# Loading the gate weights by partitions instead of by halves of their rows

## The chip, the core and the metric

The kernel runs on one core of one Trainium2 chip. The metric is the device time of one execution in microseconds (us). A core has five engines with instruction queues of their own: TensorE (PE: matmuls, and PEld: its weight loads), VectorE (DVE), ScalarE (ACT), GpSimd (POOL) and SyncE (SP). Sixteen DMA engines beside them move data between HBM and the on-chip memory SBUF, whose 128 partitions are the first axis of every tile. In this kernel DMAs are issued by SP and ACT; each of the two has a queue of its own, which the profile calls q1 (SP) and q10 (ACT).

## The reference

One decoding step of eight sequences. x is normalised; an attention over the last 2048 cached keys and values (32 query heads on 8 cached heads) gives s; a gated unit on the same normalised x gives g; the output is x + s * g. Everything stored is bfloat16.

```python
xn = _layernorm(x)                                   # 8 x 512
q = xn @ wq                                          # 32 heads of 128
scores = einsum("bhqd,bhkd->bhqk", q, k) * Dh ** -0.5    # k, v: last 2048 rows
o = einsum("bhqk,bhkd->bhqd", softmax(scores), v)
s = o.reshape(B, Sq, Hq * Dh) @ wo
h = sigmoid(xn @ w_gate) * (xn @ w_up)               # 512 x 1792 each
g = silu(h @ w_down)
return x + s * g
```

## The kernel before, in words

All that is read is some 81 MB: the weights, and for each of 8 sequences two loads of keys and two of values, 2048 KB each. Every large load fills all 128 partitions with one contiguous run per partition, which the DMA trace shows as one packet: 14336 bytes for the weights w_gate and w_up (four rows of 1792 numbers), 16384 bytes for keys and values. A DMA over 128 partitions is spread over all 16 DMA engines, eight packets on each, and each engine closes its part with a 4-byte completion write. The landing that a reader of the tile waits for is the sixteenth of these.

The order of the work is written out by hand. A list `todo` holds the loads in the order in which they are to be issued; `pump()` issues from its head as long as the pool that the load goes to has room (5 buffers for keys, 4 for values; the weights borrow these buffers), and `free()` gives a buffer back after its last reader. Nearly all loads are issued by SP (`q0`), in this order: x (L149), half of w_gate (L151), w_up, w_down and wq in two parts (L99, `load_rows`), a remainder of w_down called wd_part in three small pieces (L187), then keys and values (L89, `load_cache`), and last wo in four parts (L99). ACT (`q1`) issues two only: the other half of w_gate (L151) and a second copy of x, x4_sb (L157; the profile leaves digits out and calls it x_sb), which is needed only at the very end (L750).

What is computed from them, in order: normalisation of x (L216 to L254), the gate's 16 matmuls (L295, `hidden("wg_sb")`), its sigmoid on ACT (L308), the same 16 matmuls with w_up (L295), their product (L312), the down projection (L348; its last three matmuls need wd_part), silu (L371, L375), the queries (L385), then for each sequence the transposes of the keys (L481), scores (L500), softmax (L515 to L548) and values (L597), and at the end the output projection (L719, L733), the sum with x (L748, L750) and the store (L751).

`hidden` goes through the four rows `kt` of each partition, so that its first eight matmuls read rows 0 and 1 and its last eight rows 2 and 3. A further wait matters below: eight completion semaphores serve all DMAs in turn, so the ninth and later DMAs of SP's queue each wait until the DMA eight places before them has landed. The three wd_part pieces (L187) wait for ACT's part of w_gate, for x and for SP's part of w_gate, and the first load of keys (L89) for x4_sb, the next two for w_up and w_down.

The function that is changed, with what calls it:

Of the kernel before, what the change touches and what calls it, by code (L numbers as in the profile page):

```python
# [10 lines left out]
def kernel(  # L11
# [14 lines left out]
    P = 128  # L26
# [6 lines left out]
    KT = D // P  # L33
# [47 lines left out]
    q0, q1 = nc.sync, nc.scalar  # L81
# [65 lines left out]
    def want_first():  # L147
        t = vpool.tile([P, KT, F], bf16, name="wg_sb", tag="v")
        q0.dma_start(out=x_bf[:], in_=A_x.flatten_outer_dims())  # L149
        for q, r0 in ((q1, 0), (q0, KT // 2)):  # L150
            q.dma_start(  # L151
                out=t[:, r0 : r0 + KT // 2, :],
                in_=B_w_gate.rearrange("(p r) n -> p r n", r=KT)[
                    :, r0 : r0 + KT // 2, :
                ],
            )
        q1.dma_start(  # L157
            out=x4_sb[::S, :],
            in_=A_x.flatten_outer_dims().rearrange("b (j c) -> j b c", c=P),
        )  # L160
        for r in range(KT):
            weights[("wg_sb", r)] = t[:, r, :]

    later("v", want_first)
    want_rows("wu_sb", B_w_up, "v", KT, 0, KT)

# [38 lines left out]
    for t0, t1 in ((0, KS), (KS, 26), (26, 30), (30, RT)):  # L205
# [11 lines left out]
        out=perm[:].rearrange("k (l p) -> k l p", l=G),  # L217
        in_=ident[:].rearrange("k (p l) -> k l p", l=G),
# [13 lines left out]
        out=rstd[:], in_=mv[:, 1:2], func=AF.Sqrt, bias=eps_t[:], scale=1.0  # L232
# [4 lines left out]
        out=xn_bf[:],  # L237
# [8 lines left out]
    for kt in range(KT):  # L246
        nc.tensor.transpose(  # L247
            out=xnT_ps[:, kt, :],
            in_=xn_bf[:].rearrange("b (p kt) -> b kt p", kt=KT)[:, kt, :],
# [11 lines left out]
    for t in p_buf:  # L261
# [7 lines left out]
        out=own_q[:], in_=ident_f[:].rearrange("k (h q) -> k q h", q=NDQ), axis=AX.X  # L269
# [3 lines left out]
        out=sel_z[:], in_=ident_f[:].rearrange("k (j z) -> k z j", z=Z), axis=AX.X  # L273
# [4 lines left out]
    for p0, n, x0, x1, s0, a in PARTS:  # L278
        for x in range(x0, x1):
            nc.vector.tensor_copy(  # L280
                out=sel_part[:, x, p0 : p0 + n].rearrange("k (a e) -> k a e", a=a),
                in_=ident[:, s0 : s0 + n * (x1 - x0)].rearrange(
                    "k (e x a) -> k x a e", x=x1 - x0, a=a
                )[:, x - x0],
# [6 lines left out]
    def hidden(name):  # L291
# [21 lines left out]
        out=h_sb[:].rearrange("k t p -> k p t"),  # L313
# [7 lines left out]
        out=hT_sb[:].rearrange("k t z -> k (t z)"),  # L321
        in_=h_sb[:].rearrange("k t p -> k (t p)"),
# [79 lines left out]
    for x in range(Hkv // JQ):  # L402
        for r in range(rep):
            nc.tensor.transpose(  # L404
                out=qT_ps[:, x, r, :], in_=q_bf[:, x, r, :], identity=ident[:]
            )
        nc.vector.tensor_copy(
            out=qm_sb[:, :, x * JQ : (x + 1) * JQ, M0 : M0 + rep],
            in_=qT_ps[:, x].rearrange("d r (j z) -> d z j r", z=Z)[:, ::S],
# [11 lines left out]
    for i in range(NQ):  # L421
        nc.vector.tensor_copy(
            out=turn_rows[:].rearrange("k (i j l r) -> k i j l r", i=NQ, j=NJ, l=G)[
                :, i
            ],
            in_=ident[:].rearrange("k (l j i r) -> k i j l r", i=NQ, j=NJ, l=G)[:, i],
        )
        nc.vector.reduce_sum(
            out=sel_den[:, i * Hh : (i + 1) * Hh].rearrange("k (l r) -> k l r", l=G),
            in_=ident_f[:].rearrange("k (l j i r) -> k i l r j", l=G, j=NJ, i=NQ)[:, i],  # L430
            axis=AX.X,
        )
    for e in range(2):
        nc.vector.reduce_sum(
            out=sel_out[:, e, :].rearrange("k (i h) -> k i h", i=NQ),
            in_=ident_f[:].rearrange(
                "k (i m e h) -> k e i h m", i=NQ, m=NJ // 2, e=2
            )[:, e],
# [9 lines left out]
        out=sel_res[:],  # L448
# [6 lines left out]
        out=sel_sum[:], in_=sel_den[:].unsqueeze(2).to_broadcast([P, Hq, NDQ])  # L455
# [287 lines left out]
    for t in range(KS, RT):  # L743
# [8 lines left out]
        out=out.flatten_outer_dims().rearrange("b (j c) -> j b c", c=P),  # L752
        in_=y_bf[::S, :],
# [31 lines left out]
```

## Time and profile before

| | |
|---|---|
| Time, median of 3 runs | 199.54 us (199.35 to 199.58) |
| The profiled execution, its own time | 199.71 us |
| Its span, first to last instruction | 197.9 us |
| Busy in the span: PE, DVE, ACT, POOL | 154.0, 122.5, 37.6, 3.0 us |
| DMA: bytes, mean rate over the span | 81.32 MB, 411 GB/s |
| DMA packets; on SP's queue q1, on ACT's q10 | 6295; 6096 and 180 |
| Packet time as a share of 16 engines' span, q1 and q10 | 95.0% and 1.4% |
| Mean granted TensorE clock | 0.963 |

The profile gives the span; the 1.8 us between it and the execution's own time lie outside. A DMA issue in the timeline is the time the issuing engine spends on it, not the transfer; transfers are seen in the DMA rates, in the packets of the trace, and as releasers of those who wait. In the lines of the chain of waits the first number is the start, the second how long that piece of the chain took.

### The profile page before, as it was taken

What the parts mean: (1) busy time and instruction counts of PE and PEld (TensorE: products, weight loads), DVE (VectorE), ACT (ScalarE), POOL (GpSimd) and SP (SyncE); (2) the same over time, 40 slices, a digit from 0 to 9 for tenths busy, and PEclk for the clock granted to TensorE, in tenths of its full rate; (3) what the DMA queues carried; (4) which work ended last, traced back from release to release, by engine and by line L of the source; (5) the groups of instructions that cost most, each with busy time, mean ns of one, the idle gap of its engine ahead of it and who ended that gap; (6) DMA issues with size and microseconds to landing.
All of it is one profiled execution on the core that took longest, in us unless ns stands there. A gap on an engine that the chain in (4) does not pass through costs nothing.

```text
span 197.9 us, 4794 instructions
## 1 busy us (share of the span) xinstructions
PE 154.0 (78%) x2145; PEld 104.6 (53%) x2145; DVE 122.5 (62%) x234; ACT 37.6 (19%) x91; POOL 3.0 (2%) x11
## 2 busy tenths in 40 slices
PE   0434038799989999979798969996999897888652
PEld 0111014677676677647565646674667564566531
DVE  3754002999978678748675937685867774762301
ACT  3300011000710600240024000600060024082010
POOL 6000000000000000000000000000000000000000
PEclk9999999999999999999999969996999999999975
DMA  6999999999999999999999999999999999999980
GB/s 212 441 429 432 428 430 434 430 434 422 427 430 424 430 430 437 424 427 427 427 430 426 437 430 427 426 427 430 427 430 427 427 437 424 434 424 430 419 334 10
DMA packets 6295, 81.32 MB, mean 411 GB/s; under 512 B 764, under 2 KB 900, under 8 KB 1412
## 3 DMA queue, kind: packets, MB, share of 16 engines
q1 hardware_dynamic: 6096, 80.10, 95.0%
q10 hardware_dynamic: 180, 0.93, 1.4%
q8 instruction: 16, 0.26, 0.5%
q14 instruction: 3, 0.02, 0.0%
HBM read 81.02 MB, written 0.01 MB: 409 GB/s over the span
## 4 chain that ended last, share of the span: by engine, by line
DMA 72%; PE 22%; DVE 2%; ACT 1%; issue 1%; SPq 1%
DMA k_sb<-in_A_k_cache_dram 49%; DMA wo_sb<-in_A_wo_dram 11%; PE kT_ps L481 11%; DMA wd_part<-in_B_w_down_dram 9%; PE o_ps L597 4%; DMA wg_sb<-in_B_w_gate_dram 3%; PE s_ps L500 3%; PE q_ps L385 1%; PE fin_ps L733 1%; DVE kT_sb L486 1%; PE qT_ps L404 0%; PE b_ps L361 0%; PE pT_ps L571 0%; PE w_ps L348 0%; ACT q_bf L399 0%
## 5 line engine op out<-in xcount | busy, mean ns | idle before, releaser
L486 DVE COPY kT_sb<-kT_ps 128x1024 bf16<-128x1024 bf16 x128 | 85.2, 686 | 31.0 <-PE kT_ps L481 30.3
L481 PE MATMUL kT_ps<-perm,k_sb 128*128 128x128 bf16 x1024 | 76.5, 223 | 9.4 <-DMA k_sb<-in_A_k_cache_dram 9.3
L481 PEld LDWEIGHTS <-k_sb 128*128 128x128 bf16 x1024 | 59.7, 99 | 29.3 <-issue 16.5
L597 PE MATMUL o_ps<-v_sb,pT_sb 128*32 128x256 bf16 x512 | 39.8, 277 | 1.1 <-DVE o_sb L618 0.9
L500 PE MATMUL s_ps<-kT_sb,qm_sb 128*32 128x512 bf16 x256 | 26.0, 396 | 1.9 <-DVE kT_sb L486 1.9
L597 PEld LDWEIGHTS <-pT_sb 128*32 128x32 bf16 x512 | 22.0, 97 | 9.9 <-issue 3.3
L548 ACT ACTIVATE p_buf<-s_ps,nb 32x512 bf16<-32x512 f32 x32 | 21.7, 678 | 0.5
L541 ACT COPY nb<-m_ps 128x1 f32<-128x1 f32 x8 | 1.3, 159 | 88.3 <-PE m_ps L535 88.3
L571 PE MATMUL pT_ps<-turn_rows,p_buf 128*128 128x128 bf16 x128 | 10.9, 230 | 1.5 <-ACT p_buf L548 1.5
L564 DVE COPY pT_sb<-pT_ps 128x1024 bf16<-128x1024 bf16 x14 | 9.6, 687 | 3.9 <-PE pT_ps L571 3.9
L500 PEld LDWEIGHTS <-qm_sb 128*32 128x32 bf16 x256 | 6.7, 93 | 8.9 <-issue 2.5
L571 PEld LDWEIGHTS <-p_buf 128*128 128x128 bf16 x128 | 9.3, 150 | 3.4 <-ACT p_buf L548 2.1
L613 ACT ACTIVATE o_odd<-o_ps,own_col 128x128 f32<-128x128 f32 x8 | 2.9, 367 | 27.4 <-PE o_ps L597 27.4
L375 DVE TENSOR_TENSOR gg_sb<-sigb,b_ps 128x128 f32<-128x128 f32 x1 | 0.3, 286 | 11.7 <-ACT sigb L371 11.7
L348 PE MATMUL w_ps<-wd_part,hP_sb 52*32 52x512 bf16 (+1 forms) x3 | 0.6, 597 | 7.9 <-DMA wd_part<-in_B_w_down_dram 7.9
L548 ACT ACTIVATION_READ_ACCUMULATOR p_buf<-s_ps,nb 32x1 f32 x32 | 5.9, 184 | 0.0
L515 DVE TENSOR_REDUCE st<-s_ps 128x1 f32<-128x512 f32 x8 | 5.5, 682 | 0.5 <-PE s_ps L500 0.5
L640 DVE SCALAR_TENSOR_TENSOR own<-m_ps,inv,own_q 128x128 f32<-128x128 f32 x8 | 2.8, 346 | 3.3 <-PE m_ps L631 3.3
L348 PEld LDWEIGHTS <-hP_sb 52*32 52x32 bf16 (+1 forms) x3 | 0.1, 97 | 8.8 <-issue 8.8
L618 DVE SCALAR_TENSOR_TENSOR o_sb<-o_ps,own_col,o_odd 128x128 f32<-128x128 f32 x8 | 2.7, 339 | 3.0 <-ACT o_odd L613 3.0
L247 PE MATMUL xnT_ps<-ident,xn_bf 8*128 8x8 bf16 x4 | 0.3, 176 | 5.4 <-DVE xn_bf L236 5.4
L295 PEld LDWEIGHTS <-xnT_sb 128*32 128x32 bf16 x32 | 1.1, 119 | 6.3 <-issue 5.8
(80 smaller groups left out, 68.7 us busy)
## 6 DMA issues: line engine op xcount, KB each, us to landing
k_sb<-in_A_k_cache_dram SPq DMA_DIRECT2D x16, 2048.0 KB, 30.8
v_sb<-in_A_v_cache_dram SPq DMA_DIRECT2D x16, 2048.0 KB, 29.8
wq_sb<-in_A_wq_dram SPq DMA_DIRECT2D x2, 2048.0 KB, 18.1
wo_sb<-in_A_wo_dram SPq DMA_DIRECT2D x1, 2048.0 KB
wu_sb<-in_B_w_up_dram SPq DMA_DIRECT2D x1, 1792.0 KB, 10.5
wd_sb<-in_B_w_down_dram SPq DMA_DIRECT2D x1, 1664.0 KB, 14.0
wo_sb<-in_A_wo_dram SPq DMA_DIRECT2D x1, 1280.0 KB, 21.7
wg_sb<-in_B_w_gate_dram ACTq DMA_DIRECT2D x1, 896.0 KB
```

The lines of the kernel that those rows point to most:

```text
L385: nc.tensor.matmul(q_ps[x][Z * j : Z * (j + 1), :], lhsT=xnT_sb[:, kt, :], rhs=weights[("wq_sb", kt)][:, g * rep * Dh : (g + 1) * rep * Dh ...
L481: nc.tensor.transpose(out=kT_ps[:, c, :], in_=k_sb[:, j * CU + h * CH + c, :], identity=perm[:],)
L486: nc.vector.tensor_copy(out=kT[(b, u)][:, h * CH : (h + 1) * CH, :], in_=kT_ps[:])
L500: nc.tensor.matmul(s_ps[b][NR * l : NR * (l + 1), :], lhsT=qm_sb[:, b, i * G + l, o : o + Z], rhs=t[:, :, PG * l : PG * (l + 1)], start=(u ...
L515: nc.vector.reduce_max(out=st[b][:], in_=s_ps[b][:], axis=AX.X)
L548: nc.scalar.activation(out=p_buf[b % 2][rows, :, l, :], in_=s[rows, :].rearrange("k (c p) -> k p c", p=PG), func=AF.Exp, bias=nb[rows, :], ...
L564: copy(out=pT[b][:, h * CH : (h + 1) * CH, :], in_=pT_ps.pop(h)[:])
L571: nc.tensor.transpose(out=pT_ps[h][:, c, :], in_=p_buf[b % 2][:, :, :, h * CH + c].rearrange("k p l -> k (p l)"), identity=turn_rows[:],)
L597: nc.tensor.matmul(o_ps[rows, b % 2, :].rearrange("k (e d) -> k e d", e=2), lhsT=pT[b][:, c, rows], rhs=v[:, m, c], start=(c == 0), stop=( ...
L613: nc.scalar.mul(out=o_odd[:], in_=o_ps[:, b % 2, Dh:], mul=own_col[:, 1:2])
L618: nc.vector.scalar_tensor_tensor(out=o_of[b // 2][:, b % 2, :], in0=o_ps[:, b % 2, :Dh], scalar=own_col[:, 0:1], in1=o_odd[:], op0=ALU.mul ...
L640: nc.vector.scalar_tensor_tensor(out=own[:], in0=m_ps[:, b % 2, P : 2 * P].rearrange("p (q t) -> p q t", q=NDQ), scalar=inv[y][:, b % 2 : ...
```

## The change

Both DMAs of w_gate change their shape, and nothing else does. Before, ACT's queue carried rows 0 and 1 of all 128 partitions and SP's queue rows 2 and 3: 128 packets of 7168 bytes each. Now ACT's queue carries all four rows of partitions 0 to 111, 112 packets of 14336 bytes, and SP's queue all four rows of partitions 112 to 127, 16 packets of 14336 bytes. All other instructions keep their order on each engine. Since every row now lies in both parts, the first weight load of the gate's matmuls waits for SP's part and the first matmul for ACT's; before, the first eight matmuls waited for ACT's half alone.

```diff
-        for q, r0 in ((q1, 0), (q0, KT // 2)):
+        for q, p0, p1 in ((q1, 0, P - 16), (q0, P - 16, P)):
             q.dma_start(
-                out=t[:, r0 : r0 + KT // 2, :],
-                in_=B_w_gate.rearrange("(p r) n -> p r n", r=KT)[
-                    :, r0 : r0 + KT // 2, :
-                ],
+                out=t[p0:p1],
+                in_=B_w_gate.rearrange("(p r) n -> p r n", r=KT)[p0:p1],
             )
```

## Prediction

> **What bounds the kernel now.** I read the page's slices and chain first, then the stretches, the end of the chain, the start of the timeline, and last SP's own waits. From the page, 40 slices of 4.95 us each:
>
> ```profile
> DMA  6999999999999999999999999999999999999980
> GB/s 212 441 429 432 428 430 434 430 434 422 427 430 424 430 430 437 424 427 427 427 430 426 437 430 427 426 427 430 427 430 427 427 437 424 434 424 430 419 334 10
> ...
> DMA 72%; PE 22%; DVE 2%; ACT 1%; issue 1%; SPq 1%
> ```
>
> The reader sees transfers at 90% or more in every slice but the first and the last two, at some 428 GB/s throughout. The busy times by stretch say the same (the last two columns are DMA share and GB/s):
>
> ```profile
> 1.60:7.60 6.00, 1.23 (x12) 0.50 (x13) 3.56 (x9) 2.86 (x3) 1.90 (x6) 1.00 0.99 375
> 7.60:30.00 22.40, 7.03 (x63) 2.50 (x66) 7.27 (x18) 1.41 (x3) 0.00 (x0) 1.00 1.01 430
> 30.00:190.00 160.00, 142.63 (x2005) 99.64 (x1994) 111.05 (x206) 32.77 (x84) 0.00 (x0) 0.98 1.01 428
> ```
>
> So from 1.7 us to 190 us the DMA engines never pause; only the first 6 us run below the rate (375 GB/s). The chain of waits, from 185 us on, shows who ends last:
>
> ```profile
> 170.37 21.74 DMA wo_sb<-in_A_wo_dram
> 192.11 0.04 issue
> 192.15 1.86 PE fin_ps L733 x56
> 194.01 0.02 issue
> 194.04 0.43 PE fin_ps L733 x7
> ```
>
> The last matmuls wait for the last part of wo. Its 16 completion writes land between 190.37 and 193.99 us, and the matmuls start at 194.04. Each DMA engine has its own share of every load and none takes another's, so **the kernel ends 4 us after the slowest of the 16 engines**, and time that this engine loses anywhere, also in the first 6 us, is not made up. That makes the start of the queue the only place where this change can act. SP's waits show that the queue is fed far ahead: SP waits 124.5 us in all for buffers that the transposes free (L481), while a load of keys lands 30.8 us (median) after its issue and takes about 4.9 us of the queue (2.1 MB at 428 GB/s).
>
> **The change part by part.**
>
> *Bytes and packets.* The bytes are the same. A packet of 7168 bytes starts 0.268 us after the one before it on its engine, one of 14336 bytes 0.532 us (w_up's packets). Each engine had sixteen of the first kind and gets eight of the second: 8 x (2 x 0.268 - 0.532) = **-0.03 us**. Each engine's share is the same if 112 partitions are spread over 16 engines, seven each, as 128 are (eight each, 16 completions). The trace shows 16 engines for 128 partitions, 8 for the 8 rows of x, 5 and 4 where the outer count is 5 and 4; none for 112. If it were 14 engines with eight, those would carry nine packets with SP's one, +0.53 us. [...]
>
> *Where SP's sixteen packets go.* This is the term that decides. Every large load of before writes all 128 partitions at once. SP's new DMA writes 16 neighbouring partitions, one packet per engine, from 16 engines at once: 229,376 bytes. At the rate of all other loads it would take each engine one packet, 0.53 us. No row shows such a load, so its cost has bounds. Below: nothing more; a lead of one engine over another might even hide it. Above: if eight neighbouring partitions take no more than the one engine's rate at which they are fed in full-width loads, 16 packets go two at a time, 8 x 0.532 = 4.26 us, +3.7 us. The nearest row is the load of x (L149), the only one with many engines on few partitions: eight packets of 1024 bytes into partitions 0 to 7, from 1.687 to 1.805 us in the packet records, 8192 bytes in 0.118 us, 69 GB/s for eight partitions. Its packets took 44 ns, no more than the 46 ns of wd_part's of the same size, but its completions landed 0.36 to 0.41 us after their writes were started, against 0.33 to 0.36 us for those of ACT's half of w_gate: a first sign of queueing at 69 GB/s. I take this as the rate: 16 partitions get 139 GB/s, 229,376 bytes take 1.65 us, which is **+1.12 us** over the 0.53 us of a full-width load. Sixteen engines share the delay, and the next loads (w_up, w_down) wait behind it on each engine, since the queue is served in order.
>
> *ACT's 112 partitions.* With seven per engine, an engine's seven no longer are one group of eight; neighbours meet for one packet at each side. Below, nothing; above, two packets at half speed, +1.06 us. By the x row eight partitions take 69 GB/s, more than the 54 GB/s of two engines, so I take nothing.
>
> *When the gate weights land, and who waits.* Costed at nothing. The start of the timeline:
>
> ```profile
> 0.74 0.39 ACTq L151 DMA_DIRECT2D wg_sb<-in_B_w_gate_dram  x1
> 1.18 0.37 SPq L151 DMA_DIRECT2D wg_sb<-in_B_w_gate_dram  x1
> ...
> 7.88 0.94 PE L295 MATMUL h_ps<-wg_sb,xnT_sb 128*32 128x448 bf16 x8 [0.85 <-DMA wg_sb<-in_B_w_gate_dram]
> ...
> 8.86 0.54 ACT L308 ACTIVATE sig<-h_ps 128x448 f32<-128x448 f32 x1 [2.97 <-PE h_ps L295]
> ...
> 12.12 1.69 PE L295 MATMUL h_ps<-wu_sb,xnT_sb 128*32 128x448 bf16 x16 [3.30 <-DMA wu_sb<-in_B_w_up_dram]
> ...
> 26.75 0.61 PE L348 MATMUL w_ps<-wd_part,hP_sb 60*32 60x512 bf16 x3 [7.90 <-DMA wd_part<-in_B_w_down_dram]
> ```
>
> Now all 16 gate matmuls (2 x 0.94 = 1.88 us) wait for both parts. ACT's packets came first in before (x aside, q1's first packet on any engine starts at 4.514 us, when that engine is through with q10's); seven packets more, 3.7 us from 1.8 us with some 0.7 us lost to slow first packets, and then SP's, land at about 7.1 to 8.2 us. The gate is through by 10.1 us instead of 8.82, the sigmoid by 10.6; w_up's matmuls wait for w_up until 12.12 anyway, later if the queue is later. If SP's queue were served in turn with ACT's, ACT's part would land at about 10.3 us (1.8 + 0.7 + 14 x 0.532 + 0.35) and the gate end at 12.2; the down projection would still be done by about 20, and its last three matmuls wait for wd_part until 26.75: that is the cover, some 8 us. Without it the price would be 1.3 to 3.4 us.
>
> *The queue behind.* On SP, three pieces of wd_part wait for the two parts of w_gate and x, and behind them the first keys wait for x4_sb. x4_sb follows ACT's part in its queue and comes in eight turns with SP's packets on each of four engines, so it lands at 6.2 + 8 x 0.55 = 10.6 us or so, not 8.8. SP's first keys are then issued about 2 us later, at 11. The engines have w_up, w_down and wq before them until 25.8 us (wq's last completion), so nothing runs dry. ACT issues two DMAs as before; POOL and DVE get nothing new.
>
> **Sum.** 199.71 (this execution) + 1.12 - 0.03 = 200.8 us; the execution lies 0.17 us above the median, so the forecast is **200.6 us**.
>
> **The rivals.** About 0.2% (0.4 us) is what a measurement of this kernel can tell from no change.
>
> 1. *The sixteen packets share nothing* (27%). [...] Then only -0.03 us is left: 199.5 us. [...]
>
> 2. *Faster: the slowest engine loses its early lag* (10%). In before, ACT's first packets take 272 to 939 ns instead of 272, until about 3.6 us. The completions of ACT's half land at 4.87 to 5.32 us for fourteen engines and at 5.57 and 5.69 for the last two; for w_up it is 11.29 to 11.70, then 11.95 and 12.07. One such engine could be the one that ends last: 193.99 us, 0.35 us behind the next (193.64). If the loss is per packet, half as many packets halve it, and the two fall in with the rest: 199.54 - 0.35 - 0.03 = 199.2 us. It decides only if the sixteen packets cost less than that 0.35 us. That slow packets stop by time, not by count, on all engines, speaks against it.
>
> 3. *Harder sharing* (26%). If the engines' packets meet four to a path instead of at the x row's rate, four take 4 x 0.532 = 2.13 us, +1.6 us, and 201.1 us; with ACT's neighbours meeting too, up to +1.06 more, 202.2. For it: at 428 GB/s over 16 engines each engine always fills its own partitions at 26.8 GB/s, and nothing shows that eight partitions can take more for long. Against it: x's 69 GB/s. [...]
>
> The forecast (x's rate; 199.95 to 201.1 us) has 37%. Slower is then 37 + 26 = 63%, same 27%, faster 10%. The range leaves out the lower half of the faster case and the hardest sharing (beyond 202.2, up to the bound of +3.7 us, some 8%): 199.2 to 202.2 us.
>
> **What would show each step right or wrong.** Right: SP's sixteen 14336-byte packets, or those around them on the same engines, take clearly longer than 535 ns; the completions of w_up spread and land some 1 us after 12.07; the slice of the first 6 us falls below 375 GB/s; the last part of wo lands about 1 us after 193.99 and the chain's last matmuls start as much later, with the stretch from 30 to 190 us still at 428 GB/s. Wrong, rival 1: all those packets take 535 ns and w_up lands at 12.0. Rival 2: the same, and the last two completions of w_up close up to the rest. Rival 3: w_up lands 1.6 us late or more. The cover would be wrong if L348's last matmuls no longer waited for wd_part, and the queue if a slice after the first fell below 9 tenths. The whole reading would be wrong if w_up landed late and the last wo didn't.

## The result, and the profile after

The changed kernel takes **203.09 us** (median; 202.91 to 203.76) against 199.45 us for the kernel before measured beside it: 1.0179 times as long, 95% interval 1.0163 to 1.0195. It is slower, as forecast, but by 3.6 us instead of 1.1, and outside the range. The profiled execution took 202.91 us with a span of 200.6 us, 2.7 us more than the span of before's profiled execution, 197.9 us. That one was long: the 71 executions of before that were recorded beside the experiments have spans of 197.2 to 197.8 us, median 197.5. The changed kernel's four have 200.5 to 201.2, median 200.6. So the span grew by 3.1 us. The time outside the span differs from one execution to the next (1.7 to 3.2 us in before's, 1.8 to 3.3 in the changed kernel's).

The page's slices and chain of the changed kernel (40 slices of 5.0 us):

```profile
DMA  6999999999999999999999999999999999999980
GB/s 185 226 410 428 441 428 428 425 435 425 430 428 431 428 431 421 435 428 431 425 431 426 431 425 435 426 431 418 438 428 435 418 435 428 438 415 438 422 351 29
...
DMA 57%; PE 34%; ACT 3%; DVE 3%; SPq 1%; issue 1%
```

The reader should compare the two upper lines. The engines are as busy as before in every slice, but in the second they move 226 GB/s where before they moved 441, and in the third 410 instead of 429. From the fourth slice on both run at some 428 GB/s. Busy is the time that packets took; the packets took longer: ACT's 112 packets took 922 ns on average and 99 of them over 560, where packets of the same size (w_up's) took 535 in before. (In the last line the chain of waits now runs less over DMAs and more over PE, but the two lines above it show that the DMA engines still don't pause.) By stretches (DMA share and GB/s are the last two columns), first the changed kernel, then the kernel before for the one stretch not shown yet:

```profile
1.60:7.60 6.00, 0.29 (x4) 0.20 (x4) 3.56 (x9) 2.86 (x3) 1.90 (x6) 1.00 1.09 257
7.60:13.60 6.00, 1.69 (x16) 0.76 (x17) 4.00 (x14) 0.51 (x1) 0.00 (x0) 1.00 0.89 323
13.60:33.00 19.40, 5.93 (x55) 2.09 (x58) 3.26 (x4) 0.90 (x3) 0.00 (x0) 1.00 1.01 431
33.00:190.00 157.00, 140.02 (x1989) 98.15 (x1982) 110.05 (x204) 32.79 (x84) 0.00 (x0) 0.99 1.01 429
```

```profile
7.60:13.60 6.00, 2.42 (x24) 0.78 (x23) 4.01 (x14) 0.54 (x1) 0.00 (x0) 1.00 0.98 419
```

257 GB/s instead of 375 for 6 us are 0.71 MB too few, 323 instead of 419 another 0.58 MB: 1.28 MB in all, which at 428 GB/s are 3.0 us. That is the whole loss of the span, and it arises before 13.6 us. The start of the changed kernel's timeline:

```profile
0.74 0.40 ACTq L151 DMA_DIRECT2D wg_sb<-in_B_w_gate_dram  x1
...
1.20 0.33 SPq L151 DMA_DIRECT2D wg_sb<-in_B_w_gate_dram  x1
...
11.36 1.69 PE L293 MATMUL h_ps<-wg_sb,xnT_sb 128*32 128x448 bf16 x16 [5.66 <-DMA wg_sb<-in_B_w_gate_dram]
...
15.10 1.69 PE L293 MATMUL h_ps<-wu_sb,xnT_sb 128*32 128x448 bf16 x16 [2.06 <-DMA wu_sb<-in_B_w_up_dram]
...
29.90 0.61 PE L346 MATMUL w_ps<-wd_part,hP_sb 60*32 60x512 bf16 x3 [8.07 <-DMA wd_part<-in_B_w_down_dram]
```

w_up's matmuls start 2.98 us later than before, the matmuls that wait for wd_part 3.15 us later, and they still wait 8.07 us: nothing but the transfers has become late. In the packet records w_up's sixteenth completion lands at 15.06 instead of 12.07 us, w_down's at 18.98 instead of 16.08, wq's second at 28.64 instead of 25.78. The end of the chain:

```profile
173.08 21.88 DMA wo_sb<-in_A_wo_dram
194.96 0.04 issue
195.00 1.84 PE fin_ps L731 x56
196.84 0.00 issue
196.84 0.43 PE fin_ps L731 x8
```

The last completions of wo lie between 193.57 and 196.80 us, the last 2.81 us later than before. What the engines lost in the first 13 us they lost for good.

### The profile page after: what moved, and what is told of

Its sections match the earlier page's. It is cut to its first block, busy times and chain, and to the rows that moved or that the text cites. A ratio compares the mean times of both kernels' runs of the same rounds, so it can differ in the third digit from the quotient of the medians.

```text
span 200.6 us, 4795 instructions
## 1 busy us (share of the span) xinstructions
PE 152.2 (76%) x2145; PEld 103.8 (52%) x2145; DVE 122.2 (61%) x234; ACT 37.6 (19%) x91; POOL 3.0 (1%) x11
## 4 chain that ended last, share of the span: by engine, by line
DMA 57%; PE 34%; ACT 3%; DVE 3%; SPq 1%; issue 1%
DMA k_sb<-in_A_k_cache_dram 32%; PE kT_ps L479 17%; DMA wo_sb<-in_A_wo_dram 11%; DMA wd_part<-in_B_w_down_dram 8%; PE o_ps L595 6%; DMA wg_sb<-in_B_w_gate_dram 5%; PE s_ps L498 5%; ACT p_buf L546 2%; PE pT_ps L569 2%; PE q_ps L383 1%; PE fin_ps L731 1%; SPq L185 1%; DVE kT_sb L484 1%; ACT L546 1%; PE qT_ps L402 0%
## 5 line engine op out<-in xcount | busy, mean ns | idle before, releaser
L479 PE MATMUL kT_ps<-perm,k_sb 128*128 128x128 bf16 x1024 | 75.7, 221 | 10.5 <-DMA k_sb<-in_A_k_cache_dram 10.5
L479 PEld LDWEIGHTS <-k_sb 128*128 128x128 bf16 x1024 | 59.0, 99 | 30.1 <-issue 15.9
L293 PE MATMUL h_ps<-wg_sb,xnT_sb 128*32 128x448 bf16 x16 | 1.7, 573 | 5.7 <-DMA wg_sb<-in_B_w_gate_dram 5.7
L310 DVE TENSOR_TENSOR h_sb<-sig,h_ps 128x448 bf16<-128x448 f32 x1 | 2.1, 2077 | 4.9 <-PE h_ps L293 4.9
```

What stands on the lines that cost most here:

```text
L293: nc.tensor.matmul(ps[Z * j : Z * (j + 1), :], lhsT=xnT_sb[:, kt, :], rhs=weights[(name, kt)][:, j * FC : (j + 1) * FC], start=(kt == 0), ...
L310: nc.vector.tensor_tensor(out=h_sb[:].rearrange("k t p -> k p t"), in0=sig[:, :FC].rearrange("k (p t) -> k p t", t=FT), in1=u_ps[:].rearra ...
L479: nc.tensor.transpose(out=kT_ps[:, c, :], in_=k_sb[:, j * CU + h * CH + c, :], identity=perm[:],)
```

## The experiments

The most telling number of each run is when w_up's last completion lands, since all of the gate's load is ahead of it: 12.07 us in before. It is read from one execution, the traced one. Spans of one kernel mostly differ by 0.2 to 0.7 us, and before's traced one was 0.4 us longer than its median, so small differences between landings don't count by themselves; the median span of all executions is given where it matters. Times are medians; each ratio is against the kernel before on the same chip.

| run | gate's load | w_up landed, us | time, us | ratio, 95% interval |
|---|---|---|---|---|
| before | two halves of the rows | 12.07 | 199.45 | |
| changed | 112 and 16 partitions, two queues | 15.06 | 203.09 | 1.0163 to 1.0195 |
| e1 | 128 partitions, one load on ACT | 12.44 | 199.97 | 1.0020 to 1.0048 |
| e2 | 112 and 16, both on SP | 15.41 | 203.01 | 1.0156 to 1.0195 |
| e3 | 64 and 64, two queues | 15.81 | 203.22 | 1.0150 to 1.0289 |
| e4 | 112 alone | 13.80 | 200.99 | 1.0056 to 1.0098 |
| e12 | e4's bytes over 128 partitions | 11.57 | 199.24 | 0.9960 to 1.0001 |
| e5 | before, and 16 neighbours | 13.70 | 201.23 | 1.0062 to 1.0119 |
| e6 | before, and 16, eight apart | 12.69 | 200.22 | 1.0014 to 1.0051 |
| e7 | before, and 16, seven apart | 12.69 | 199.96 | 1.0012 to 1.0040 |
| e8 | before, and the same bytes over 128 | 12.51 | 199.82 | 1.0013 to 1.0038 |
| e9 | 112 as seven loads of 16 | (see there) | 210.68 | 1.0537 to 1.0588 |
| e10 | 128 partitions, one load on SP | 12.70 | 200.42 | 1.0041 to 1.0074 |
| e11 | one load for each row | 12.07 | 199.77 | 1.0006 to 1.0034 |

**e1, one full-width load** in place of the loop over two.

```diff
+        q1.dma_start(out=t[:], in_=B_w_gate.rearrange("(p r) n -> p r n", r=KT))
```

> All of w_gate in one load of 128 partitions with packets of 14336 bytes on ACT's queue; SP's queue starts with w_up. Theory A (engines that write few neighbouring partitions at once share a path into SBUF): no load is narrow any more, so the time is that of before, 199.4 us within 0.4, w_up lands at about 12.0 us, and the packets from 4 us on take 535 ns. Theory B (two queues served in turn cost time): w_up's packets now take turns with ACT's, so it is slow, 201 us or more. Theory C (large packets at the cold start cost time): slow too, above 201 us.

Theory B falls, and C as the whole cause: two queues in turn with large packets lose 0.37 us at w_up, not 3. But 199.97 us is more than A's 199.4 within 0.4, and the median span is 198.0 us against 197.5: a small part of the loss, 0.37 of 2.99 us at w_up, 0.5 of 3.1 us in the span, comes with this one large load. All but two of w_up's 128 packets took 535 ns or 2 ns less.

**e2, both loads on one queue.** Only `q1` becomes `q0`, so that SP issues both.

> The changed kernel's two loads (112 and 16 partitions), both on SP's queue, one behind the other. Theory A: still slow, 201.0 to 202.5 us, w_up lands 1.5 to 2.5 us after 12.07; a little less than with two queues since the narrow load no longer mixes with the rest. Theory B: back to 199.4 us. Theory C: as slow as the changed kernel, 203 us.

203.01 us and w_up at 15.41: as slow as the changed kernel. With e1, the split by partitions is the cause, not the second queue. The loss is larger than A's expected 1.5 to 2.5 us.

**e3, halves of the partitions.**

```diff
+        for q, p0, p1 in ((q1, 0, P // 2), (q0, P // 2, P)):
```

> Partitions 0 to 63 on ACT's queue, 64 to 127 on SP's, packets of 14336 bytes, four of each per engine. Theory A: sixteen engines write only half of the partitions, two engines to each path; served one after the other each packet takes twice as long, 8.5 us instead of 4.3, so 203 to 204 us; less (down to 201.5) where the two queues are served in turn. If only the sixteen-partition load is a burden: 199.4 us. Theories B and C: 203 us, as the changed kernel.

203.22 us, +3.74 us at w_up: within A's 203 to 204. (One of the four executions took 206.16 us, so the interval is wide.) ACT's 64 packets took 990 ns on average in place of 535, and none took less than 560; SP's 64 behind them took 1070 on average, which is twice 535, as theory A had it. A load need not be as narrow as 16 partitions to be slow.

**e4, the 112 partitions alone.** SP's load is left out; the gate's matmuls read 112 partitions.

> ACT's 112 partitions alone; the load of partitions 112 to 127 and their share of the gate's sum (64 of 512 rows) are left out, so 0.53 us less per engine is to be moved than in before. If the sixteen partitions alone cause the loss, as the prediction took it: 198.9 us, w_up at 11.5 us. Theory A with neighbours meeting (two packets per engine at half speed): 199.5 to 200.2 us, w_up at 12.3 to 12.9 us. If most of the loss is in the 112: 201 us or more.

200.99 us, w_up at 13.80: later than theory A's 12.3 to 12.9. Most of the loss is here, where the prediction had put nothing. The median span, 199.1 us, says the same.

**e12, the control for e4**, run last, with the same bytes over the full width.

```diff
+        part = 7 * F // 2
+        q1.dma_start(
+            out=t[:].rearrange("p r n -> p (r n)")[:, :part],
+            in_=B_w_gate.rearrange("(p r) n -> p (r n)", r=KT)[:, :part],
+        )
```

> The control for e4: the same 1.6 MB of w_gate in one load on ACT's queue, but full width: the first 12544 bytes (three and a half rows) of all 128 partitions, eight packets per engine instead of seven of 14336. Left out are the last half row and its two matmuls (two of sixteen). If the loss of e4 comes from 112 partitions not being dealt out as 128 are (theory A): no loss but that of the cold start, w_up at 11.8 to 12.0 us (e1's 12.44 less 0.53), 199.3 to 199.6 us. If it comes from the bytes, the queue or the packet size: w_up at 13.8 and 201.0 us as in e4.

w_up at 11.57 us against 13.80, and 199.24 against 200.99 us: the same number of bytes on the same queue is 2.23 us later at w_up, and 1.75 us longer in time and in the median span (199.1 against 197.35), when it goes to 112 partitions and not to 128. The packets of e12 are smaller (12544 bytes), but e1's had e4's 14336 bytes, and it lost 0.37 us. The stretches show it, e4 first, then e12:

```profile
1.60:7.60 6.00, 0.29 (x4) 0.30 (x5) 3.56 (x9) 2.86 (x3) 1.90 (x6) 1.00 1.00 274
7.60:13.60 6.00, 1.68 (x16) 0.64 (x16) 4.01 (x14) 0.54 (x1) 0.00 (x0) 1.00 0.99 351
```

```profile
1.60:7.60 6.00, 0.29 (x4) 0.31 (x5) 3.27 (x9) 2.86 (x3) 1.67 (x6) 1.00 0.96 360
7.60:13.60 6.00, 3.36 (x30) 1.27 (x30) 4.58 (x15) 0.54 (x1) 0.00 (x0) 1.00 1.01 429
```

Both have a DMA share of about 1; e4 moves 274 and 351 GB/s with it, e12 360 and 429. In e4, 107 of ACT's 112 packets took over 560 ns, the 112 took 839 on average, and 92 of w_up's 128 behind and between them took over 560 ns too.

**e5 to e8, what partitions a load of 16 goes to.** Each adds to the kernel before one load behind SP's half of w_gate, 131,072 bytes into a tile `extra` that nothing reads; e5, e6 and e7 read the same rows of HBM.

```diff
+        q0.dma_start(out=extra[P - 16 : P], in_=G[P - 16 : P, :4096])      # e5
+        q0.dma_start(out=extra[0:121:8], in_=G[P - 16 : P, :4096])         # e6
+        q0.dma_start(out=extra[0:106:7], in_=G[P - 16 : P, :4096])         # e7
+        q0.dma_start(out=extra[:, :512], in_=G[:, :512])                   # e8
```

(G is w_gate as partitions by 7168 numbers.)

> The kernel before with one more load behind SP's half of w_gate, into a tile that nothing reads: 8192 bytes to each of the 16 partitions 112 to 127, one packet per engine (0.31 us of each engine at the usual rate). Theory A1 (eight neighbours share a path): eight packets to a path, 2.4 us, w_up lands at 14.2 us instead of 12.07, 201.5 us. [...] Theory D (the sixteen packets are slow because they read neighbouring rows of HBM): slow as well, and by the same amount in the two runs that read the same rows into other partitions. No sharing: 12.4 and 199.7 us.

> As e5, the same rows of HBM, but into partitions 0, 8, 16 to 120. Theory A1: every packet has a path of its own: 12.4 us for w_up's landing, 199.7 us, all packets at some 310 ns. [...] Theory D: as slow as e5.

> As e5, the same rows of HBM, but into partitions 0, 7, 14 to 105. [...] Theory D: as slow as e5.

> As e5 with the same number of bytes, as 1024 bytes to each of all 128 partitions: what 0.13 MB more cost when nothing meets. All theories: w_up at 12.4 us, 199.7 us.

Against e8, with the same number of bytes, e5's load into neighbours costs 1.41 us more and e6's into partitions eight apart 0.40 (from the times). e7's, seven apart, is 0.14 us above e8, with almost the same interval: in time alone the two can't be told apart. Median spans, which scatter less, are 199.25, 198.3, 198.15 and 198.0 us for e5, e6, e7 and e8. e5 to e7 read the same rows and differ, so theory D, the reading side, falls. The start of w_up's matmuls, e5 and then e8:

```profile
13.74 1.68 PE L298 MATMUL h_ps<-wu_sb,xnT_sb 128*32 128x448 bf16 x16 [4.05 <-DMA wu_sb<-in_B_w_up_dram]
```

```profile
12.56 1.68 PE L298 MATMUL h_ps<-wu_sb,xnT_sb 128*32 128x448 bf16 x16 [3.70 <-DMA wu_sb<-in_B_w_up_dram]
```

The packet records give the pattern. Of the sixteen packets of 8192 bytes, 309 ns each at the usual rate, e5's took 309 to 1038 ns, e6's 309 to 528, and e7's 309 but for one of 456. Theory A1 (a path for each eight neighbours) expected some 310 for all of e6's, w_up at 12.4 and 199.7 us, and e6 gave 12.69 and 200.22: it falls. For e5 its 14.2 and 201.5 us were too much, by 0.5 and 0.3: 13.70 and 201.23. What the sixteen share, and what that costs, isn't settled. That e6's packets, eight partitions apart, were slower than e7's, seven apart, would be hard to explain by neighbourhood alone. In their landings e6 and e7 don't differ (12.69 both).

The harm doesn't end with the sixteen: the first 24 packets of w_up behind them took up to 1669 ns in e5, 1001 in e6 and still 709 in e7, against 535 (one of 581) in e8. In e7 the sixteen themselves were hardly slowed, yet w_up's packets were. Why, no record shows.

**e9, 112 as seven loads.**

```diff
+        for i in range(7):
+            q1.dma_start(out=t[i : P - 16 : 7], in_=G[i : P - 16 : 7])
```

(here G is w_gate as partitions by rows.)

> As e4 (112 partitions alone, the share of the other 16 left out), but as seven loads on ACT's queue of 16 partitions each, seven apart: load i takes partitions i, i+7 to i+105, so that engine e gets partition 7e+i, one at a time. If the single load of 112 gives engine e the partitions 7e to 7e+6 in order, the loss is that of e4: w_up at 13.8 us, 201.0 us. If the single load deals its partitions out in another way, with more meeting on a path: less, w_up at 12.5 to 13 us, 199.5 to 200.3 us. If it isn't the meeting of engines at all but the number 112 in one load: w_up at 11.9 us, 199.3 us.

The time is of no use, for a reason of the kernel's own. Its timeline:

```profile
0.74 29.24 ACTq L151 DMA_DIRECT2D wg_sb<-in_B_w_gate_dram  x7
...
30.08 1.11 ACTq L152 DMA_DIRECT2D x_sb<-in_A_x_dram  x1
```

The seven loads took ACT 29 us to issue. The last two of the seven waited for the two parts of wq on SP's queue, which landed at 22.69 and 29.44 us, and ACT's square root waited behind them, until 32.52 us, and with it the whole normalisation. The 210.68 us say nothing on how the single load deals out its partitions.

The transfers do say something. The first five of the seven loads went out beside w_up and w_down:

```profile
1.60:7.60 6.00, 0.00 (x0) 0.00 (x0) 1.41 (x5) 0.00 (x0) 1.90 (x6) 1.00 0.96 300
7.60:13.60 6.00, 0.00 (x0) 0.00 (x0) 0.00 (x0) 0.00 (x0) 0.00 (x0) 1.00 0.99 289
```

All 80 packets of these five took over 560 ns, 845 on average, where e4's took 839; without the first sixteen of each, at the start, it is 780 and 772. No load here has 112 partitions, so the number 112 in one load is not what makes packets slow. Loads of partitions seven apart do it too, as they would if the single load gave each engine seven neighbours in order; that it does so isn't shown, nor that engine e gets partition 7e+i of load i.

**e10 and e11, the size of the first packets.** e10 is e1 with `q0` for `q1`; e11 loads each row by itself, rows 0 and 1 on ACT's queue, 2 and 3 on SP's, in packets of 3584 bytes.

> All of w_gate in one load of 128 partitions on SP's queue, with w_up behind it. If the 0.37 us that w_up landed late in e1 came from large packets at the cold start (theory C, small): the same again, w_up at 12.3 to 12.5 us, 199.8 to 200.0 us. If it came from two queues in turn (theory B, small): 12.0 us and 199.4.

> Full-width loads of one row each, packets of 3584 bytes: rows 0 and 1 on ACT's queue, 2 and 3 on SP's. If large packets cost time at the cold start, smaller ones may save some: w_up at 11.7 to 12.0 us, 199.1 to 199.4 us. More packets cost about 5 ns each, 16 more per engine 0.08 us. If the loss at the start goes by time or bytes and not by packets: 12.1 us, 199.5 us.

e10's 12.70 us and 200.42 us repeat e1's small loss, and more than was expected, with only the 8 KB of x4_sb on ACT's queue: two queues in turn aren't needed for it. That the size of the first packets makes it isn't shown. e11 turns small packets into no gain: w_up lands at 12.07 as in before, and 199.77 us is slightly slower. (The 5 ns expected for each further packet lie between what before's 7168- and 14336-byte packets show by their starts, 2 x 268 - 532 = 4 ns, and by their durations, 2 x 272 - 535 = 9.) And e12, with 12544 bytes to a packet, landed w_up at 11.57 us, earlier than expected; with the 0.53 us for the bytes that it leaves out that is 12.10, no loss by the landing. Of the full loads of w_gate tried here, that of before is the fastest.

## Why the prediction was wrong, point by point

*What bounds the kernel* held. The loss of the first 13 us reappears at the end almost whole, 2.99 us at w_up and 2.81 at the last wo, at an unchanged rate between (428 and 429 GB/s from 33 to 190 us). That no engine takes another's share fits before's records: the two completions that came last in w_up, at 11.95 and 12.07 us, with the fourteenth at 11.70, are as far behind in wq's second part, 25.65 and 25.78 with the fourteenth at 25.39. That the slowest engine decides was not put to the test, since all sixteen lost.

*Bytes and packets* (-0.03): sixteen engines were used, as taken, with sixteen completions for the 112 partitions. The sign was wrong: one full-width load in packets of 14336 bytes cost +0.37 us at w_up and +0.5 us in the median span (e1). Its first sixteen packets took 772 to 2180 ns where before they took 272 to 939 ns for half the bytes; whether their size is the reason stays open (e11, e12).

*SP's sixteen packets* (+1.12): that they cost more than their bytes was right; that the size is near is in part luck. By themselves e5's packets, of only 8192 bytes, lost 1.19 us at w_up against their control; in proportion 14336 bytes would lose some 2.1 us (an estimate), more than the 1.12 from x's rate. In the changed kernel, where ACT's packets beside them were slow already, the step from e4 is 15.06 - 13.80 = 1.26 us, of which 0.53 is the time of the bytes that e4 leaves out: +0.73, or +0.97 by the median spans.

*ACT's 112 partitions* (0, at most +1.06) is **the step that failed**. "By the x row eight partitions take 69 GB/s, more than the 54 GB/s of two engines, so I take nothing": measured, 13.80 us (e4) against 12.44 - 0.53 = 11.91 (e1 less the bytes left out) is +1.89 us, and against the direct control e12 +2.23; by the median spans it is 1.6 and 1.75. Two things were wrong in it. x's eight packets were not slowed at all (44 ns, beside 46 for wd_part's of the same size), so 69 GB/s is the rate at which 8 KB came in a tenth of a microsecond, and no limit for a load of 1.6 MB. And the upper bound counted meetings of neighbours within the load only, at most two of an engine's seven packets, an estimate of mine that no record shows; in e4 107 of 112 packets were stretched, and w_up's with them. The three terms, 0.37 + 1.89 + 0.73, give the 2.99 us that w_up was late; they do so by the way they are formed, so the sum confirms nothing, but in each way of counting the 112 partitions have the largest part.

*When the gate lands, and who waits*: right in its conclusion. ACT's part landed later than either estimate, at 11.31 us instead of 7.1 to 8.2 or, in turns, 10.3, and the two queues' packets were in fact mixed, though not from the start: SP's sixteen packets started between 5.82 and 6.59 us, after 79 of ACT's 112, and 31 of ACT's started after the last of them. The cover held: the matmuls behind wd_part still waited 8.07 us.

*The queue behind*: right in its conclusion. x4_sb landed at 15.32 us, later than the 10.6 expected, SP issued the first keys at 15.34, and wq filled the engines until 28.64.

*The rivals.* No sharing (199.5) is refuted by e5 against e8, 201.23 against 199.82 us for the same number of bytes. Rival 2, the slowest engine's early lag: the lag did close up (w_up's last two completions are 15.03 and 15.06 behind 14.95, and wo's last two 196.79 and 196.80), but all engines had lost more. Rival 3, four to a path and 112's neighbours meeting, came nearest in time; its 202.2 us were still 0.9 us short, for the same term. No run shows four packets on a path, its +1.6 us; in its place the runs showed 1.19 us at w_up for e5's sixteen packets and 0.73 for SP's sixteen beside the 112. x's row, by which I set it second, was weak evidence: 8 KB.

*Open.* Which partitions each engine gets of a load of 112 was not seen, since the packet records name neither engines nor partitions. That packets of several engines share a path, theory A, is argued from e3, e5 to e7, e9 and e12; the path itself isn't shown. Of the 3.64 us between the median times 3.1 us are in the span; the other half microsecond lies outside it and is less than what the time outside differs by from one execution to the next, so it can't be told from scatter. And why every other full-width load of the whole of w_gate that was tried is a little slower than before's two halves (e1, e10, e11) stays open.

## What to carry to other kernels

Where the DMA engines bound a kernel, as here (a DMA share of 1.01 from 33 to 190 us), a load that fills all 128 partitions is worth keeping at that width; if it must be cut, the runs speak for cutting along the bytes of a partition (199.45 us in two halves of the rows, 199.77 row by row) and against cutting along the partitions (203.09 at 112 and 16, 203.22 at 64 and 64). Look at the packets' durations, not at the busy share: a share of 100% looks the same at 257 as at 428 GB/s. A bound on an unknown cost should come from a row of like size: the nearest in shape was here 200 times too small.

## What the runs showed of the hardware that was not expected

A load over 64 partitions, issued beside one over the other 64, was as bad as 112 and 16 (e3: 231 GB/s from 1.6 to 7.6 us against 375). Sixteen packets of 8192 bytes were enough to stretch packets of the next load to as much as three times their 535 ns (1669 in e5). Where the sixteen went mattered: 201.23 us into neighbours, 200.22 and 199.96 us into partitions eight and seven apart, and 199.82 us for the same number of bytes over all 128.
